# Delta-rule attention and a gated layer on one core: weight staging, a split of the recurrence's vector work, and a new instruction order

## The chip, the cores and the metric

The kernel runs on one core of a Trainium2 chip. The time is the device time of one execution in microseconds, of which the median of three runs is given. A core has the engines TensorE (PE in the profile, its weight loads PEld), VectorE (DVE), ScalarE (ACT), GpSimd (POOL) and SyncE (SP). Each executes its own instructions in order; SyncE, ScalarE and GpSimd also issue DMAs from their instruction streams, where an issue that has to wait holds up what stands behind it.

## The reference

```python
# q, k, v: (4, 8, 768, 48); beta: (4, 8, 768)
k_n = k / (np.linalg.norm(k, axis=-1, keepdims=True) + 1e-06)
for t in range(S):                       # state: (B, H, 48, 48), zero at first
    y[:, :, t] = q[:, :, t] @ state      # per batch and head
    v_old = state.T @ k_n[:, :, t]
    state += beta_t * outer(k_n_t, v_t - v_old)
x = y.transpose(0, 2, 1, 3).reshape(3072, 384)
h = x @ w_in                             # (384, 2048), float64 as given
out = (h * np.cos(h)) @ w_out            # (2048, 384), float64 as given
```

## The kernel before

**Tiling.** The sequence of 768 steps is cut into 24 units of 32 steps; a unit holds all four batches on 128 partitions (four quarters of 32) and eight heads beside each other. Two units make a pair of 256 tokens, the tile of the gated layer; there are 12 pairs.

**A unit of the recurrence** runs through: load k, q, v; transpose k and q (`turn`, units 0 to 5 on PE, later by `blocks` DMAs and a DVE transpose); Gram products of keys with keys and queries (`gram`); scale by beta over the squared norm (`gram_keys`), mask (`gram_queries`); invert the unit triangular matrix; then `through_state` (L930, k and q times the state), `right_side` (L947), `solve` (L1002), `solve_out` (L1014, which writes u twice, once for each half of the partitions' parity, by two multiplications with `bz`), `update` of the state (L1027) and `update_out` (L1035), `within` (L1045 for units 0 and 1, L1057 for later ones), `within_out` (L1070, four copies on ACT), `features` (L1078, transposes to tokens) and `features_out`.

**The inverses.** Units 0 and 1 are inverted by repeated multiplication on PE (`double`, L759, six levels with a copy on ACT, L767, and transposes and additions on DVE, L775, L772 and L779, between them). From unit 2 on the Gram block goes through DRAM (`gram_put`, L833; `gram_get`, L846/L854), is inverted column by column on GpSimd (L879, L886), and comes back through DRAM (`put`, L891; `get`, L902/L910). Units 2 and 3 are inverted in half blocks, with `solve_half` (L960), `between` and a last `solve` in place of one solve.

**The norms** of a pair's keys: a square on ACT (L557), a reduction on DVE (L562), a square root on GpSimd (L574), and five to six small DVE instructions (L591 to L598 for pairs 0 to 2, L603 to L611 later) that make `bs` and `bz`; `weigh` (L628) multiplies v by the norm.

**The gated layer.** Pair 0 is computed plainly: `hidden` (L1099) makes 512 hidden rows of 128 tokens as one block of 12 products, eight blocks in all; the gate takes two ACT (L1136, L1152) and two DVE instructions (L1143, L1155) for each; `output` (L1297) is eight blocks of four products. Later pairs use sums of weight and feature tiles to save products (`layer`, L1273; `product`, L1355), with sums of weight tiles made once by `in_sums` (L1235) and `right_sum` (L1384).

**The weights** arrive as float64 in 28 tiles (12 of w_in, 512 KB each; 16 of w_out, 384 KB each). `narrow_load` (L518) puts a tile into one of the eight g_ffn buffers, the same eight that hold gates, key squares and half solutions. Its words are turned into float32 by two ACT instructions (`split`, L528 and L532), one of DVE (`shift`, L536) and one of GpSimd (`add`, L540). A hidden block needs the adds of its tiles.

**The order.** Every step is a task with its engine; a list of task numbers, `Order.LINE`, written out in the source, fixes the order in which all tasks are issued, and so the order on each engine. The set `Order.OTHER` names tasks that run on their second engine: for a DMA the ScalarE queue in place of SyncE's, for a sum GpSimd and DVE exchanged. Costs and due times stand beside the tasks but only the list decides. Warm-up products (`keep_warm`, L495) are tasks like the others. Buffers are taken and given back in the list's order.

Of the kernel before, what the change touches and what calls it, by code (L numbers as in the profile page):

```python
# [10 lines left out]
FP = mybir.dt.float32  # L11
# [13 lines left out]
def _consts():  # L25

    p = np.arange(128)
    share = p // 64
    row = SPLIT * np.arange(C // SPLIT)[None, :] + share[:, None]
    return np.concatenate(
        [
            np.eye(128),
            p[:, None] % C < np.arange(C)[None, :],
            p[:, None] // C % 2 == np.arange(2)[None, :],
            p[:, None] // 16 % 2 == np.arange(2)[None, :],  # L40
            -1.0 * (p[:, None] // C % 2 == np.arange(2)[None, :]),
            (row[:, :, None] == np.arange(C)).reshape(128, -1),
        ],
        axis=1,
    ).astype(np.float32)


def _masks():
# [3 lines left out]
    other = ~side  # L52
    return np.concatenate(
        [(t < i) & (t // half == i // half), t // half < i // half]
        + [(s & x[:, None, :]).reshape(128, 2 * C) for s, x in ((side, t == i), (other, t < i))],
# [4 lines left out]
class Order:  # L60

    OTHER = {
        ('v', 0), ('v', 1), ('gram_put', 2), ('gram_put', 3), ('inv', 1, 0), ('put', 1),
        ('gram_put', 4), ('v', 5), ('gram_get', 2), ('put', 2), ('gram_put', 6), ('v', 8),
        ('v', 9), ('blocks', 9, 0), ('blocks', 9, 1), ('put', 4), ('get', 10), ('v', 11),
        ('blocks', 11, 0), ('blocks', 11, 1), ('gram_put', 11), ('gram_get', 5), ('v', 12),
        ('gram_put', 13), ('gram_get', 6), ('get', 13), ('v', 14), ('blocks', 14, 0), ('v', 15),
        ('blocks', 15, 0), ('blocks', 15, 1), ('v', 16), ('gram_put', 16), ('v', 17), ('k', 18),
        ('v', 18), ('get', 18), ('v', 20), ('gram_put', 21), ('gram_get', 11), ('store', 0, 1),
        ('right', 4, 4), ('left', 1, 1, 0), ('left', 1, 3, 0), ('left', 1, 3, 1),  # L70
        ('store', 1, 0), ('store', 1, 1), ('x_sum', 2, 'd'), ('x_sum', 2, 'n'),
        ('x_sum', 2, 'm'), ('x_sum', 2, 'e'), ('x_sum', 2, 'k'), ('x_sum', 2, 'g'),
        ('x_sum', 2, 'i'), ('x_sum', 2, 'l'), ('x_sum', 2, 'f'), ('x_sum', 2, 'b0'),
        ('left', 2, 4, 1), ('left', 2, 3, 1), ('x_sum', 3, 'd'), ('x_sum', 3, 'n'),
        ('x_sum', 3, 'm'), ('x_sum', 3, 'e'), ('x_sum', 3, 'k'), ('x_sum', 3, 'g'),
        ('x_sum', 3, 'i'), ('x_sum', 3, 'l'), ('x_sum', 3, 'h'), ('x_sum', 3, 'b0'),
        ('left', 3, 4, 1), ('left', 3, 3, 1), ('store', 3, 0), ('store', 3, 1),
        ('x_sum', 4, 'd'), ('x_sum', 4, 'm'), ('x_sum', 4, 'g'), ('x_sum', 4, 'i'),
        ('left', 4, 3, 0), ('left', 4, 3, 1), ('x_sum', 5, 'd'), ('x_sum', 5, 'e'),
        ('x_sum', 5, 'l'), ('x_sum', 5, 'h'), ('x_sum', 5, 'b0'), ('left', 5, 2, 0),  # L80
        ('left', 5, 4, 1), ('left', 5, 3, 0), ('left', 5, 3, 1), ('x_sum', 6, 'd'),
        ('x_sum', 6, 'g'), ('x_sum', 6, 'l'), ('x_sum', 6, 'f'), ('x_sum', 6, 'b0'),
        ('left', 6, 1, 0), ('left', 6, 4, 0), ('store', 6, 0), ('x_sum', 7, 'd'),
        ('x_sum', 7, 'm'), ('x_sum', 7, 'g'), ('x_sum', 7, 'i'), ('x_sum', 7, 'f'),
        ('x_sum', 7, 'h'), ('x_sum', 7, 'b0'), ('left', 7, 4, 0), ('left', 7, 4, 1),
        ('left', 7, 3, 1), ('store', 7, 0), ('x_sum', 8, 'd'), ('x_sum', 8, 'm'),
        ('x_sum', 8, 'e'), ('x_sum', 8, 'k'), ('x_sum', 8, 'g'), ('x_sum', 8, 'l'),
        ('left', 8, 3, 0), ('store', 8, 0), ('store', 8, 1), ('x_sum', 9, 'd'),
        ('x_sum', 9, 'm'), ('x_sum', 9, 'e'), ('x_sum', 9, 'k'), ('x_sum', 9, 'i'),
        ('x_sum', 9, 'l'), ('x_sum', 9, 'b0'), ('left', 9, 1, 0), ('left', 9, 2, 0),  # L90
        ('left', 9, 1, 1), ('left', 9, 3, 0), ('store', 9, 1), ('x_sum', 10, 'k'),
        ('x_sum', 10, 'i'), ('x_sum', 10, 'l'), ('x_sum', 10, 'h'), ('x_sum', 10, 'b0'),
        ('left', 10, 1, 0), ('left', 10, 1, 1), ('left', 10, 4, 1), ('left', 10, 3, 0),
        ('left', 10, 3, 1), ('store', 10, 1), ('x_sum', 11, 'd'), ('x_sum', 11, 'e'),
        ('x_sum', 11, 'k'), ('x_sum', 11, 'g'), ('x_sum', 11, 'f'), ('left', 11, 1, 0),
        ('left', 11, 2, 0), ('left', 11, 1, 1), ('left', 11, 3, 0), ('left', 11, 3, 1),
        ('store', 11, 1), ('store_right', 11), ('weights', 2), ('weights', 3), ('weights', 4),
        ('weights', 9), ('weights', 11), ('weights', 12), ('weights', 13), ('weights', 14),
        ('weights', 15), ('weights', 17), ('weights', 23), ('weights', 24)
    }  # L100

    WARM_FIRST, WARMS = 5, 17
    LINE = """
# [1845 lines left out]
```

## Time and profile before

| | |
|---|---|
| three runs | 640.14, 640.42, 641.46 us; median 640.42 |
| profiled execution, its own time | 642.77 us |
| its span, first to last instruction | 641.0 us |
| mean granted TensorE clock | 0.98 |
| HBM read and written | 38.95 MB and 10.22 MB |
| DMA packets | 215844, of them 207384 under 512 B |

A row of the timeline gives start and duration in microseconds, the engine, the source line, the operation, its output and input tiles with partitions x elements, a count, and in brackets the time for which the engine was idle before it and what released it. ACTq and SPq are the DMA issues in the streams of ScalarE and SyncE. A product in float32 leaves two records on PE, so a hidden block of 12 products is "x24". A row of groups (by line) gives the busy time, the mean in ns, and the idle time ahead. A row of windows gives a stretch, its length, then the busy time and the count for PE, PEld, DVE, ACT and POOL, the granted clock, the share of DMA time and GB/s. Ends of matmuls are modelled, so a busy PE is not PE at its peak.

### The profile page before, as it was taken

What the parts mean: (1) busy time and instruction counts of PE and PEld (TensorE: products, weight loads), DVE (VectorE), ACT (ScalarE), POOL (GpSimd) and SP (SyncE); (2) the same over time, 40 slices, a digit from 0 to 9 for tenths busy, and PEclk for the clock granted to TensorE, in tenths of its full rate; (3) what the DMA queues carried; (4) which work ended last, traced back from release to release, by engine and by line L of the source; (5) the groups of instructions that cost most, each with busy time, mean ns of one, the idle gap of its engine ahead of it and who ended that gap; (6) DMA issues with size and microseconds to landing.
All of it is one profiled execution on the core that took longest, in us unless ns stands there. A gap on an engine that the chain in (4) does not pass through costs nothing.

```text
span 641.0 us, 24058 instructions
## 1 busy us (share of the span) xinstructions
PE 612.1 (95%) x10096; PEld 571.4 (89%) x10096; DVE 504.4 (79%) x1051; ACT 297.5 (46%) x533; POOL 435.1 (68%) x791
## 2 busy tenths in 40 slices
PE   6978788999999999999999999999999999999997
PEld 4857777788799998999999999999999999999997
DVE  5876736999999897788878788978878676757872
ACT  3546535645543543543743553643544443635440
POOL 4428877788888888786886786888884881212231
PEclk8897979999999999999999999999999999999999
DMA  9876656655354645446234445333225011000001
GB/s 187 218 169 174 136 130 134 148 87 83 72 87 74 103 74 96 69 67 111 42 52 87 75 79 91 54 45 70 45 35 101 18 31 23 20 3 15 13 20 30
DMA packets 215844, 50.75 MB, mean 79 GB/s; under 512 B 207384, under 2 KB 210744, under 8 KB 215736
## 3 DMA queue, kind: packets, MB, share of 16 engines
q1 hardware_dynamic: 161132, 32.34, 27.8%
q10 hardware_dynamic: 54300, 16.33, 12.1%
q8 instruction: 79, 1.29, 0.8%
q0 software_dynamic: 304, 0.54, 0.4%
q14 instruction: 29, 0.24, 0.1%
HBM read 38.95 MB, written 10.22 MB: 77 GB/s over the span
## 4 chain that ended last, share of the span: by engine, by line
PE 76%; DMA 8%; POOL 5%; DVE 5%; issue 2%; SPq 2%; ACT 1%; ACTq 1%; DVEq 0%; POOLq 0%
PE p_out L1355 30%; PE p_h L1273 28%; PE p_kq L930 3%; PE p_s L1027 3%; POOL part L879 2%; POOL z L886 2%; PE p_u L1002 2%; PE p_kq L1057 2%; PE p_g L675 2%; PE p_h L1099 2%; DMA qp<-in_q_dram 2%; PE p_h L1355 2%; DMA kp<-in_k_dram 2%; PE p_z L1078 1%; DMA w_sum<-z_dr 1%
## 5 line engine op out<-in xcount | busy, mean ns | idle before, releaser
L879 POOL TENSOR_TENSOR part<-z,gb 128x126 f32<-128x126 f32 (+23 forms) x321 | 141.6, 441 | 44.1 <-DMA gb<-g_dr 17.5
L886 POOL TENSOR_TENSOR z<-z,part 128x126 f32<-128x126 f32 (+23 forms) x321 | 142.8, 445 | 25.2
L1355 PE MATMUL p_out<-w_out,g_ffn 128*128 128x192 f32 x672 | 121.0, 329 | 0.0
L1355 PEld LDWEIGHTS p_out<-w_out,g_ffn 128*128 128x128 f32 x672 | 107.9, 190 | 1.0
L1152 ACT ACTIVATE turns<-turns,halfpi 128x512 f32<-128x512 f32 x96 | 68.0, 718 | 83.2 <-DVE turns L1143 71.6
L1273 PE MATMUL p_h<-x_sum,w_in 128*128 128x128 f32 x704 | 92.3, 278 | 0.0
L1355 PE MATMUL p_out<-w_sum,g_ffn 128*128 128x192 f32 x496 | 88.7, 328 | 0.0
L1273 PEld LDWEIGHTS p_h<-x_sum,w_in 128*128 128x128 f32 x704 | 85.6, 191 | 1.9
L1136 ACT ACTIVATE turns<-g_ffn,quarter_turn 128x512 int32<-128x512 f32 x77 | 55.0, 719 | 66.3 <-DVE g_ffn L1155 35.4
L1355 PEld LDWEIGHTS p_out<-w_sum,g_ffn 128*128 128x128 f32 x496 | 79.6, 190 | 0.6
L1290 DVE TENSOR_TENSOR g_ffn<-g_ffn,p_h 128x512 f32<-128x512 f32 x88 | 59.5, 679 | 14.7 <-PE p_h L1273 13.7
L1155 DVE TENSOR_TENSOR g_ffn<-turns,g_ffn 128x512 f32<-128x512 f32 x77 | 61.7, 810 | 11.7 <-ACT turns L1152 11.6
L1143 DVE SCALAR_TENSOR_TENSOR turns<-g_ffn,turns 128x512 f32<-128x512 f32 x77 | 57.1, 750 | 8.2 <-ACT turns L1136 8.1
L1273 PE MATMUL p_h<-x_sum,in_sum 128*128 128x128 f32 x440 | 58.9, 278 | 0.8 <-POOL x_sum L1188 0.8
L1273 PEld LDWEIGHTS p_h<-x_sum,in_sum 128*128 128x128 f32 x440 | 54.3, 191 | 2.2 <-POOL x_sum L1188 1.0
L1070 ACT COPY y<-p_kq 32x384 f32<-32x384 f32 x96 | 45.1, 470 | 19.0 <-PE p_kq L1057 8.1
L1407 DVE SCALAR_TENSOR_TENSOR o<-p_out,o 128x192 f32<-128x192 f32 x74 | 25.1, 351 | 29.7 <-PE p_out L1355 29.5
L1273 PE MATMUL p_h<-x_ffn,w_in 128*128 128x128 f32 x352 | 46.6, 277 | 1.0 <-ACT p_h L1285 1.0
L1273 PEld LDWEIGHTS p_h<-x_ffn,w_in 128*128 128x128 f32 x352 | 43.0, 192 | 1.6 <-ACT p_h L1285 1.3
L574 POOL TENSOR_TENSOR knrm<-ksum,halves 128x16 f32<-128x16 f32 (+1 forms) x14 | 37.1, 2647 | 10.1 <-DVE ksum L562 9.5
L1371 POOL TENSOR_TENSOR g_ffn<-g_ffn 128x512 f32<-128x512 f32 x15 | 19.1, 1271 | 30.5 <-DVE g_ffn L1155 26.6
L1285 ACT COPY p_h<-p_h 128x512 f32<-128x512 f32 x44 | 25.3, 575 | 28.5 <-PE p_h L1273 20.4
(168 smaller groups left out, 1051.7 us busy)
## 6 DMA issues: line engine op xcount, KB each, us to landing
g_ffn<-in_moe_w_in_dram SPq DMA_DIRECT2D x7, 512.0 KB, 7.8
g_ffn<-in_moe_w_out_dram SPq DMA_DIRECT2D x9, 384.0 KB
kp<-in_k_dram SPq DMA_DIRECT2D x136, 24.0 KB, 2.5
gb<-g_dr SPq DMA_DIRECT2D x12, 256.0 KB, 3.9
g_ffn<-in_moe_w_out_dram ACTq DMA_DIRECT2D x7, 384.0 KB
g_ffn<-in_moe_w_in_dram ACTq DMA_DIRECT2D x5, 512.0 KB, 5.9
vp<-in_v_dram ACTq DMA_DIRECT2D x52, 48.0 KB, 2.7
zt<-z_dr SPq DMA_DIRECT2D x68, 32.0 KB, 2.7
```

Source lines behind the costliest of these rows:

```text
L574: nc.gpsimd.tensor_tensor(out=scales[m][2][:, part], in0=sums[m, part.start][:, 0:n], in1=halves[:, 0:n], op=ALU.pow,)
L879: eng.tensor_tensor(out=part, in0=z[:, 0:rows, j, None].to_broadcast(shape), in1=a[:, j, None, j + 1 :].to_broadcast(shape), op=ALU.mult,)
L886: eng.tensor_tensor(out=behind, in0=behind, in1=part, op=ALU.subtract)
L1070: nc.scalar.copy(by_parity(y[quarter(b)]), p_kq[quarter(b ^ 1), :, b % 2])
L1136: nc.scalar.activation(turns[p, f], hidden_of(p, f), AF.Identity, bias=quarter_turn, scale=TURN)
L1143: nc.vector.scalar_tensor_tensor(out=r, in0=hidden_of(p, f), scalar=TURN, in1=t, op0=ALU.mult, op1=ALU.subtract,)
L1152: nc.scalar.activation(r, r, AF.Sin, bias=halfpi, scale=2.0 * math.pi)
L1155: nc.vector.tensor_tensor(out=place(p, f), in0=step_of(rests.pop((p, f)), f), in1=step_of(hidden_of(p, f), f), op=ALU.mult,)
L1273: nc.tensor.matmul(p_h[:, e], in_block(*w)[:, e], x_of(p, b), start=new and e == 0, stop=True, skip_group_check=True,)
L1285: nc.scalar.copy(to, part_of(p, one))
L1290: nc.vector.tensor_tensor(out=part_of(p, to), in0=part_of(p, one), in1=part_of(p, two), op=op)
L1355: nc.tensor.matmul(p_o, left(p, part, a)[:, e % 4], right(e, b), start=(e == 0), stop=(e == FT // 2 - 1), skip_group_check=True,)
```

## The change

**Weight staging.** Tiles 0 to 5 (of w_in) and 12 to 15 (of w_out) are loaded into the place that w_out will fill; tiles 16 to 27 into w_sum, once unit 1 has been solved; only tiles 6 to 11 still use g_ffn buffers. Loads and splits wait for the adds of tiles that were staged in the same place.

```diff
+    def stage_of(t):
+        if t < 6:
+            return "out", 1024 * t, 1024 * t + 1024
+        if t < 12:
+            return None
+        if t < 16:
+            return "out", 3072 + 768 * (t - 12), 3840 + 768 * (t - 12)
+        return "sum", 768 * (t % 4), 768 * (t % 4) + 768
...
     def narrow_load(t):
-        words[t] = g_home("pairs", t).bitcast(U32)[:, 0 : 2 * n]
+        words[t] = staged(t).bitcast(U32)[:, 0 : 2 * n]
```

**Pair 0 in pieces.** `hidden` becomes four tasks of three products each, `output` four tasks of one product each for every former block. The products are the same.

```diff
-            add(layered[0], "PE", 2.62, lambda f=f: hidden(p, f), deps,
+            for i in range(4):
...
+                add(layered[0], "PE", 0.66, lambda f=f, i=i: hidden(p, f, i), deps,
```

**Norms.** From pair 1 on, the square and its sum over 48 columns are one ACT instruction per unit and head with an accumulator (8 or 16 instructions); the reduction on DVE goes. ACT also squares the norm plus 1e-6 and copies the norms for `weigh` (`norms_out`); DVE keeps the reciprocal and one product.

```diff
+        if m > 0:
+            for i in range(n):
+                for h in range(H):
+                    nc.scalar.activation(
+                        square, kps[m % len(kps)][:, part.start + i, h, 0:D], AF.Square,
+                        accum_out=ksum[:, i, h : h + 1],
+                    )
+            return
...
+        nc.scalar.activation(krec, knrm, AF.Square, bias=tiny)
```

**u.** From unit 2 on, DVE writes u once (one instruction instead of two, half the elements); `within` reads it, and two ACT instructions make the two copies that `update` reads. `within` no longer waits for `update`.

```diff
+    def part_out(n):
+        u = parts[n] = work.tile([128, H, 2, D], FP, name="u", bufs=1)
+        for x in range(2):
+            nc.scalar.activation(u[:, :, x], us[n], AF.Copy, scale=odd[:, x : x + 1])
```

**Smaller edits.** Units 0, 1, 4 and 5 are solved in quarters (32 products of 32x48 in place of 16 of 64x48), and units 0 and 1 use the same quarter form of `within` as the others, with one DVE instruction for the masked queries instead of two. `double_rest` is cut into `double_eye` and `double_far`, of which unit 0's two and unit 1's second run on GpSimd. `right_side` has three DVE instructions instead of four. For units 0 to 3 half of `within_out` is a task of its own (`within_half`, on DVE for units 0 and 1, on ACT for 2 and 3). The identity of the GpSimd inverse is read from a 62-column constant that is loaded later, from SyncE. The table load of ACT stands behind four instead of eight DMA issues. Three sums of weight tiles go to GpSimd, and ten of eleven feature sums of pair 1 to DVE.

**The order.** `Order.LINE` and `Order.OTHER` are new lists; 22 instead of 17 warm-up tasks, besides the five at the start. In ScalarE's stream the first DMA issue behind the loads of k and q stands now behind the first five weight splits; the loads of weights 0 to 6, of v and the gram stores of units 2 to 5 are issued by SyncE, put 1 by ScalarE. The split of weight tile 1 stands ahead of unit 0's first doubling copies, the split of tile 2 ahead of its second ones. On PE, unit 0's six levels are no longer interleaved evenly with those of unit 1, whose last three levels come after unit 0's solve. `features` 0 follows `within` 0 directly, and hidden pieces stand in runs of one to five between the steps of units 1 to 3.

475 lines of the change are left out of this document (269 added, 206 removed), and 204 rows, old and new, of the table LINE.

## The prediction

> **What bounds the kernel now.** I read the profiled execution by stage first: the busy totals, then a table of windows (columns: length, busy time and count of PE, PEld, DVE, ACT, POOL, clock, DMA share, GB/s).
>
> ```profile
> span 641.0 us, 24058 instructions
> PE 612.1 (95%) x10096; PEld 571.4 (89%) x10096; DVE 504.4 (79%) x1051; ACT 297.5 (46%) x533; POOL 435.1 (68%) x791
> ```
> ```profile
> 6.00:58.70 52.70, 40.62 (x928) 34.15 (x926) 41.11 (x123) 29.05 (x59) 24.07 (x27) 0.87 0.78 193
> 58.70:112.00 53.30, 43.74 (x1057) 40.14 (x1052) 31.48 (x66) 26.24 (x52) 42.82 (x82) 0.90 0.64 139
> 112.00:190.00 78.00, 76.75 (x1245) 64.18 (x1247) 74.81 (x145) 40.38 (x73) 66.33 (x116) 1.00 0.54 95
> 190.00:640.00 450.00, 446.37 (x6878) 429.04 (x6870) 354.22 (x708) 201.85 (x350) 297.77 (x557) 1.00 0.32 55
> ```
>
> Two regimes. From 112 us on TensorE is idle 1.3 us up to 190 and 3.6 us from there to the end, at full clock: there only TensorE's own work can shorten the run. From 6 to 112 us it is idle 12.1 + 9.6 = 21.7 us, with a mean clock of 0.87 and 0.90. All that this change can win lies ahead of 112 us, where the first units' recurrence runs as one chain through PE, DVE, ACT and the DMA queues and too little feed-forward work is ready to fill the holes. Whatever the chain gains there, the packed rest starts earlier by.
>
> The next view is the order of time in that head; start, duration, engine, and in brackets the idle time before and its releaser.
>
> ```profile
> 17.98 2.21 ACTq L398 DMA_DIRECT2D vp<-in_v_dram  x3
> ...
> 21.52 0.69 ACT L528 ACTIVATE w_in<-g_ffn 128x512 f32<-128x512 f32 x1 [3.26 <-DMA vp<-in_v_dram]
> ...
> 43.27 2.17 ACTq L833 DMA_DIRECT2D g_dr<-g  x2
> 45.48 0.37 ACT L767 COPY in_sum<-p_h 128x256 f32<-128x256 f32 x1 [7.37 <-DVE w_in L536]
> ```
> ```profile
> 25.93 1.96 PE L759 MATMUL p_h<-in_sum 64*64 64x128 f32 x32
> ...
> 46.89 1.32 PE L1002 MATMUL p_u<-vp,in_sum 64*64 64x48 f32 x32 [0.30 <-ACT kq_t L652]
> ...
> 58.71 4.75 PE L1099 MATMUL p_h<-x_ffn,w_in 128*128 128x128 f32 x24
> 63.40 1.13 PE L1002 MATMUL p_u<-rhs,w_sum 64*64 64x48 f32 x32
> ...
> 82.71 1.54 PE L960 MATMUL p_w<-rhs,w_sum 32*32 32x48 f32 x60 [0.81 <-DMA w_sum<-z_dr]
> ...
> 86.30 4.62 PE L1099 MATMUL p_h<-x_ffn,w_in 128*128 128x128 f32 x24
> 90.85 0.88 PE L996 MATMUL p_u<-g_ffn,w_sum 32*32 32x48 f32 x64
> 91.66 2.94 PE L1099 MATMUL p_h<-x_ffn,w_in 128*128 128x128 f32 x24
> 94.53 0.89 PE L1027 MATMUL p_s<-u,kp 64*64 64x96 f32 x32
> ...
> 99.48 1.15 PE L930 MATMUL p_kq<-st,kq_t 48*64 48x48 f32 x64
> ```
>
> Twice ScalarE stands still behind DMA issues in its own instruction stream (3.26 and 7.37 us) while copies of the doubling chain wait behind them; solve 0 comes at 46.89 us, the first hidden block at 58.71. Later, whole blocks of 12 products (24 records, 2.94 us at full clock, 4.62 and 4.75 at half) stand between the short steps of units 2 and 3: between their correction and their solve, and between solve and state update.
>
> **The change part by part.** I write the steps as a sum against the profiled 642.77 us (span 641.0, 1.8 outside it); the median shown is 640.42, 2.35 less.
>
> *Up to solve 1.* The weights no longer wait for a g_ffn buffer, so they go out from SyncE's queue and the two early stalls of ScalarE's queue go; the matrices of two inverse steps go to GpSimd; one unit's bz and half of two queries leave DVE. Against that stand the following prices.
>
> ```profile
> L536 DVE TENSOR_SCALAR w_in<-w_in 128x512 uint32<-128x512 uint32 x12 | 4.8, 411 | 0.0
> L562 DVE TENSOR_REDUCE ksum<-g_ffn 128x8 f32<-128x384 f32 (+1 forms) x6 | 4.1, 682 | 5.4 <-ACT g_ffn L557 5.4
> L779 DVE TENSOR_TENSOR in_sum<-in_sum,p_h 128x256 f32<-128x256 f32 x8 | 3.3, 412 | 3.1 <-PE p_h L759 2.1 <-ACT in_sum L767 1.0
> ...
> L775 DVE STREAM_TRANSPOSE in_sum<-p_h 128x256 f32<-128x256 f32 x6 | 2.7, 443 | 0.7 <-PE p_h L759 0.6
> ...
> L628 DVE SCALAR_TENSOR_TENSOR vp<-knrm,vp 128x768 f32<-128x768 f32 x2 | 1.9, 968 | 1.3 <-DMA qp<-in_q_dram 1.3
> ```
> ```profile
> L528 ACT ACTIVATE w_in<-g_ffn 128x512 f32<-128x512 f32 x12 | 8.2, 684 | 4.6 <-DMA vp<-in_v_dram 3.3 <-DMA qp<-in_q_dram 0.7 <-POOL part L879 0.6
> L528 ACT ACTIVATE w_out<-g_ffn 128x384 f32<-128x384 f32 x12 | 6.6, 549 | 0.0
> L652 ACT COPY kq_t<-p_t 128x512 f32<-128x512 f32 x12 | 6.4, 588 | 6.0 <-PE p_t L642 3.9 <-DMA g_ffn<-in_moe_w_in_dram 2.1
> ```
> ```profile
> 8.21 0.20 ACT L461 ACTIVATE warm<-halfpi 128x1 f32<-128x1 f32 x1
> ...
> 48.13 0.87 ACT L557 ACTIVATE g_ffn<-kp 128x768 f32<-128x768 f32 x1
> ```
> ```profile
> g_ffn<-in_moe_w_in_dram SPq DMA_DIRECT2D x7, 512.0 KB, 7.8
> ```
>
> In the new order of ScalarE the split of weight tile 1 stands ahead of the first copies of the doubling. Its load is issued near 11 us; with 7.8 us to landing and two halves of some 0.65 it ends near 20, so the second level starts at 20.6 us. Before the third level stand a copy of k and q (1.2), eight squares (1.6, below), another split (1.3) and a copy (0.4) on ScalarE, then turn 3 (1.1) on PE: the third level starts near 28.7, where the old one started at 25.93, so 2.8 us later. From there to the last addition DVE is the chain: seven transposes at 0.44, eight additions and two products of gram blocks of the same size at 0.41, four shifts at 0.41, one weigh (0.97), and five small ones of a fold and a scale that I put at 1.3 together: 11.1 us in all, from 30.3 to 41.4. Solve 0 follows at about 42.2 against 46.89: -4.7. The old stretch from the third level to solve took 21 us because of the 7.37 us stall and because both inverses were carried side by side. After solve 0 the new order puts update, within and features directly behind; half of the copy of y goes to DVE, so the first hidden piece comes near 49 against 58.71. But 5.5 us of unit 1's doubling, turn 4, gram 4 and state 1 are then still ahead, so the gain that holds is that at solve 1: I get 58.5 against 63.40. **-5** for this stage, between 0 (should the early weight tile come 5 us later than its median) and -8.
>
> *The squares with a sum on ScalarE.* A pair's one square (0.87) and its sums on DVE (0.68 in the mean) become 16 activations of 48 columns with an accumulator, not in the trace of before. From below they cost 0.13 each, the slope between 128x256 and 128x512 rows carried to 48 columns; from above 0.37, the 128x256 copy. I take 0.20, the nearest row (128x1): 3.2 us instead of 0.87. In the head eight of them stand on the chain twice (counted above); in the packed stage ScalarE is busy 201.85 of 450 us and takes 2.3 more per pair, 1.9 for the split of u (two activations of 384 columns per unit) and 0.9 for small copies: some 5 us in 44, which its idle half hides. Were that cover gone, PE would wait up to 2.3 us per pair, 23 us over ten pairs; I take +0.5.
>
> The Trainium skill's page "ScalarE: Activation LUTs", section "What ACT_TABLE_LOAD costs", gives 186 ns + 0.833 ns per column with some 93 ns of overlap; by it 16 squares take an estimated 2.2 us, and the sum would differ by under 1 us. Its "Rules for kernel authors" gives additions and products to VectorE, which speaks against this part; the trace says that DVE, 74.81 busy of 78 us between 112 and 190, is the fuller of the two.
>
> *Units 2 and 3.* The inverse of unit 2 arrives by eight DMAs that stand behind a gram store in SyncE's queue.
>
> ```profile
> 71.98 5.06 SPq L902 DMA_DIRECT2D w_sum<-z_dr  x8
> ```
>
> That order stays, so p_w of unit 2 moves with the chain, from 82.71 to about 78. Behind it the hidden work comes in pieces of three products (0.73 us). Between the correction and solve 2 one piece remains of 4.5 us of block, saving 3.7; between solve and update two pieces and the new u copy (1.0) replace 2.94 and a 1.0 us u: saving 0.5 to 1; and the 2.94 us block that stood behind the update ahead of state 3 goes, within now standing before update: 2. State 3 then stands at 88 to 90 against 99.48. Unit 3 repeats it, but from there PE runs out of holes: between 49 us and solve 3, I count some 42 us of PE work in the new order, so the chain's further lead is capped by PE. What counts is the idle time removed: of 9.6 us between 58.7 and 112, I take back 6, of the half-clock loss (two blocks by 1.7 us each) 1.5. The rest stays, as the inverse of units 4 and 5 (30 us of GpSimd) starts only 2.5 us earlier. **-7.5**, between -2 and -11.
>
> *TensorE's own work.*
>
> ```profile
> 66.43 1.51 PE L1045 MATMUL p_kq<-u,zt 64*64 64x96 f32 x32
> ...
> 95.36 0.88 PE L1057 MATMUL p_kq<-u,tt 32*32 32x48 f32 x64
> ```
> ```profile
> 134.86 1.16 PE L1273 MATMUL p_h<-x_sum,in_sum 128*128 128x128 f32 x8
> 135.85 1.06 PE L1273 MATMUL p_h<-x_ffn,w_in 128*128 128x128 f32 x8
> 136.75 1.06 PE L1273 MATMUL p_h<-x_ffn,in_sum 128*128 128x128 f32 x8
> ```
>
> Two within steps take 64 small records instead of 32 wide ones, -0.6 each, and four solves likewise, -0.25 each: -2.2. A layer behind another shape starts its successor after 0.99 us, behind its own shape after 0.90, so a change of shape costs 0.1; the pieces add about 22 such changes among hidden and 8 among output: +3. The five more warm-up products only fill idle time. **+0.8.** DVE's savings in the packed stage (some 3 us a pair) are worth nothing there, as PE is the bound.
>
> Sum: -5 - 7.5 + 0.8 + 0.5 = -11.2, of which I keep 10 (the steps overlap where PE is already full): 632.8 for the profiled execution, 630.4 against the median. **I predict 630.5 us.**
>
> **The rivals.** (1) *Little gain*: the early weight tiles delay ScalarE's copies (the split standing in front) and the crowded DMA (share 0.78 between 6 and 58.7) delays k and q, and solve 1 stays near 63; what units 2 and 3 win is given back where solve 4 waits for GpSimd's inverse, which starts hardly earlier: 635 to 641. For it: 7.8 us to landing; against it: buffers free from the start. (2) *Slower*: ScalarE becomes the serial engine. If the 16 squares take over 0.3 us each (4.8 us a pair, and 10 us with the rest), they push part_out, which now stands between solve and update, and the layer copies; the update is placed in PE's order as if they were short, and PE waits. It decides from about 1 us of wait per unit on: 20 units, +20, less 10 from the head, gives 650. Against it: PE waited for ACT hardly at all after 190 us. (3) *Packed head*: from 49 us on PE has no hole and stays at full clock: 582 us of the old run lie behind its first hidden block, less 12 idle, 5 of half clock and 1 of work, plus 5.5 us of work moved behind it: about 571 after 49, thus 620 and the median at 619. For it: pieces of 0.73 us fit any hole. (4) The change does what it says, by the built order; that isn't in doubt.
>
> ```profile
> 84.00:88.00 4.00, 3.38 (x84) 3.07 (x74) 1.47 (x4) 2.58 (x5) 3.30 (x10) 0.50 0.92 274
> ```
>
> Half clock was granted right behind the long holes, as in this row behind the wait for z_dr. The Trainium skill's "TensorE: Matmul & The Clock Gate", Part 1, says that an idle window of about 3.4 us brings the half rate and a sustained busy one ends it; by that rule rival 3 takes its 5 us back as well, and the trace agrees so far.
>
> **How the numbers follow.** Forecast (-5 to -16 us) 0.60; little gain 0.16, of which a third within 0.2%; packed 0.12; slower 0.12. A measurement of this kernel can tell 0.2% (1.3 us) from no change. Faster: 0.60 + 0.12 + 0.10 = 0.82; same 0.06; slower 0.12. The range leaves out half of the packed case and the slower one: 619 to 642. The likeliest case alone spans 624 to 635.
>
> **What would show it.** Right: solve 0 at 40 to 44 us, the first hidden piece before 51, solve 1 near 58.5, state 3 before 91, no ACT idle over 3 us before a doubling copy, idle PE under 13 us between 6 and 112, and from 112 on PE as full as now. Wrong: doubling copies waiting for a split; squares over 0.3 us; idle PE named after ACT u behind 190 us; PE waiting for zt at solve 4 by more than 3 us.

## The result and the profile after

The changed kernel takes 647.56 us in the median of seven runs (646.38 to 653.62), the kernel before 641.26 (637.67 to 644.14): ratio **1.011**, interval 1.007 to 1.015. It is slower by 1.1%; 630.5 us was forecast. The profiled execution took 646.41 us, that of before 642.77.

First the page's totals of the kernel after, then its windows with the same borders as in the prediction (length, busy time and count of PE, PEld, DVE, ACT, POOL, clock, DMA share, GB/s).

```profile
span 644.6 us, 24744 instructions
...
PE 613.1 (95%) x10296; PEld 568.4 (88%) x10296; DVE 475.1 (74%) x931; ACT 374.1 (58%) x950; POOL 429.7 (67%) x787
...
6.00:58.70 52.70, 42.24 (x1033) 36.34 (x1033) 40.62 (x107) 37.40 (x122) 32.71 (x43) 0.97 0.85 206
58.70:112.00 53.30, 46.45 (x1168) 39.27 (x1161) 36.29 (x67) 37.03 (x106) 42.97 (x75) 0.97 0.64 130
112.00:190.00 78.00, 75.36 (x1409) 63.65 (x1411) 70.06 (x132) 50.82 (x137) 63.55 (x115) 1.00 0.56 100
190.00:640.00 450.00, 443.59 (x6688) 425.49 (x6689) 324.98 (x614) 247.34 (x588) 286.93 (x546) 1.00 0.31 53
```

Length less PE's busy time is its idle time. Up to 112 us it fell from 12.08 + 9.56 to 10.46 + 6.85 us: **-4.3**. Behind 112 us it was 1.25 + 3.63 before, of which 2.66 lie behind the last product (the old run ends at 641.0 with 3.65 us of tail), so 2.2; after it is 2.64 + 6.41 = 9.05 with no tail in it: **+6.8**. Busy time rose by 1.0, start and tail by 0.2. Together +3.7, and the span grew by 3.6.

Busy time alone hides the clock, which differs between the two traces. PE was granted half clock in these stretches, first before, then after:

```profile
11.33:21.57 10.24, 7.11 (x124) 5.77 (x124) 9.21 (x27) 2.20 (x6) 4.57 (x6) 0.50 0.82 174
55.70:62.53 6.83, 6.83 (x105) 6.19 (x102) 5.25 (x16) 4.16 (x9) 5.58 (x17) 0.50 0.66 176
83.01:89.84 6.83, 6.21 (x138) 5.90 (x134) 2.15 (x7) 2.58 (x5) 5.58 (x17) 0.50 0.89 254
```
```profile
16.06:19.48 3.42, 3.42 (x90) 3.12 (x85) 2.38 (x8) 2.64 (x10) 3.19 (x3) 0.50 0.78 141
108.22:111.64 3.42, 3.42 (x11) 2.21 (x10) 2.23 (x5) 3.24 (x15) 2.87 (x8) 0.50 1.06 273
384.70:388.12 3.42, 3.42 (x14) 3.42 (x14) 1.74 (x3) 1.82 (x3) 3.33 (x4) 0.50 0.34 54
```

An estimate from them: a hidden block of 24 records takes 2.94 us at full clock and 4.75 at half, so a busy microsecond at half clock is worth 0.62 at full. At full clock PE's work would then be 604.5 us before and 609.2 after: **+4.7**, not +1.0. The slower clock cost 5.1 us less up to 112 us and 1.3 more behind it. The balance of the two traces is then, in the head, -4.3 idle and -5.1 clock; behind 112 us, +6.8 idle and +1.3 clock; in PE's own work, wherever it lies, +4.7; start and tail, +0.2.

So the change is ahead at 112 us: PE has 519.7 us of busy time left there (75.36 and 443.59, and 0.80 behind 640 us), and the kernel before 523.1. It loses the lead behind 112 us, where it stands idle for 6.8 us more.

The medians differ by 6.3 us, 2.7 more than the traced executions. The clock can account for that: the kernel before had a mean granted clock of 0.987 in 74 executions beside the experiments and 0.980 in the traced one, the change 0.989 in 13 executions and 0.992 in the traced one. So most of the clock's gain belongs to the two executions that were traced.

The order of time on PE (start, duration, engine, line, operation, output and inputs, and in brackets the idle time ahead with its releaser):

```profile
41.19 0.88 PE L1039 MATMUL p_u<-vp,in_sum 32*32 32x48 f32 x64 [0.80 <-DVE in_sum L822]
...
48.69 0.91 PE L1159 MATMUL p_h<-x_ffn,w_in 128*128 128x128 f32 x6
...
58.55 0.29 PE L1039 MATMUL p_u<-rhs,w_sum 32*32 32x48 f32 x8
...
88.17 1.15 PE L965 MATMUL p_kq<-st,kq_t 48*64 48x48 f32 x64
...
383.65 1.16 PE L1333 MATMUL p_h<-x_sum,in_sum 128*128 128x128 f32 x8 [1.94 <-ACT p_h L1345]
384.64 2.70 PE L1414 MATMUL p_out<-w_sum,g_ffn 128*128 128x192 f32 x8
387.14 1.52 PE L1333 MATMUL p_h<-x_ffn,w_in 128*128 128x128 f32 x8
388.50 1.47 PE L1414 MATMUL p_out<-w_sum,g_ffn 128*128 128x192 f32 x8
```

Solve 0 at 41.19 (46.89 before, 42.2 forecast), first hidden piece at 48.69 (58.71; 49), solve 1 at 58.55 (63.40; 58.5), state 3 at 88.17 (99.48; 88 to 90). Every milestone came within about 1 us of the forecast, and the kernel is slower. The last four rows show a new sight, a layer that waits 1.94 us for a copy on ScalarE; behind the wait one block of eight products takes 2.70 us, where the next takes 1.47.

What PE waited for behind 112 us (in total, times, longest), first after, then before:

```profile
PE p_h L1333 <- ACT p_h L1345: 2.6, 2, 1.9
PE p_out L1414 <- DVE o L1466: 2.0, 4, 1.0
PE p_h L1333 <- ACT g_ffn L1345: 1.1, 3, 0.7
PE p_u L1044 <- DMA zt<-z_dr: 1.0, 2, 0.8
```
```profile
PE p_h L1273 <- ACT p_h L1285: 1.0, 1, 1.0
PE p_h L1273 <- POOL x_sum L1188: 0.8, 1, 0.8
```

And what ScalarE did ahead of the 1.94 us, with its two groups for the squares (count, busy time, mean ns, idle time ahead):

```profile
L587 ACT ACTIVATE square<-kp 128x48 f32<-128x48 f32 x176 | 42.7, 243 | 6.5 <-DMA kp<-in_k_dram 1.4
L587 ACT ACTIVATION_READ_ACCUMULATOR square<-kp 128x1 f32 x176 | 32.8, 187 | 0.0
...
376.66 0.25 ACT L587 ACTIVATE square<-kp 128x48 f32<-128x48 f32 x1
376.81 0.19 ACT L587 ACTIVATION_READ_ACCUMULATOR square<-kp 128x1 f32 x1
377.03 0.24 ACT L587 ACTIVATE square<-kp 128x48 f32<-128x48 f32 x1
...
382.17 0.24 ACT L587 ACTIVATE square<-kp 128x48 f32<-128x48 f32 x1
...
383.02 0.57 ACT L1345 COPY p_h<-p_h 128x512 f32<-128x512 f32 x1
```

An activation with an accumulator is two instructions, and one square comes every 0.37 us (376.66, 377.03): the 16 of a pair hold ScalarE for 5.9 us in one piece, and the copy that PE needs stands behind them.

### The profile page after: what moved, and what is told of

Its sections match the earlier page's. It is cut to its first block, busy times and chain, and to the rows that moved or that the text cites. A ratio compares the mean times of both kernels' runs of the same rounds, so it can differ in the third digit from the quotient of the medians.

```text
span 644.6 us, 24744 instructions
## 1 busy us (share of the span) xinstructions
PE 613.1 (95%) x10296; PEld 568.4 (88%) x10296; DVE 475.1 (74%) x931; ACT 374.1 (58%) x950; POOL 429.7 (67%) x787
## 5 line engine op out<-in xcount | busy, mean ns | idle before, releaser
L914 POOL TENSOR_TENSOR part<-z,gb 128x126 f32<-128x126 f32 (+23 forms) x321 | 139.9, 436 | 37.9 <-ACT z L902 9.9
L1414 PE MATMUL p_out<-w_sum,g_ffn 128*128 128x192 f32 x496 | 90.0, 331 | 1.7 <-DVE o L1466 1.7
L1215 DVE TENSOR_TENSOR g_ffn<-turns,g_ffn 128x512 f32<-128x512 f32 x77 | 57.4, 751 | 12.7 <-ACT turns L1212 12.6
L1116 ACT COPY y<-p_kq 32x384 f32<-32x384 f32 x88 | 41.4, 470 | 13.3 <-PE p_kq L1103 7.1
L1430 POOL TENSOR_TENSOR g_ffn<-g_ffn,g_ffn 128x512 f32<-128x512 f32 x12 | 16.2, 1354 | 48.1 <-PE p_out L1414 28.1
L587 ACT ACTIVATE square<-kp 128x48 f32<-128x48 f32 x176 | 42.7, 243 | 6.5 <-DMA kp<-in_k_dram 1.4
L1333 PEld LDWEIGHTS p_h<-x_ffn,w_in 128*128 128x128 f32 x352 | 44.4, 194 | 2.3 <-ACT p_h L1345 1.0
```

The costliest lines, as they stand in the source:

```text
L587: nc.scalar.activation(square, kps[m % len(kps)][:, part.start + i, h, 0:D], AF.Square, accum_out=ksum[:, i, h : h + 1],)
L914: eng.tensor_tensor(out=part, in0=z[:, 0:rows, j, None].to_broadcast(shape), in1=a[:, j, None, j + 1 :].to_broadcast(shape), op=ALU.mult,)
L1116: nc.scalar.copy(by_parity(y[quarter(b)]), p_kq[quarter(b ^ 1), :, b % 2])
L1215: nc.vector.tensor_tensor(out=place(p, f), in0=step_of(rests.pop((p, f)), f), in1=step_of(hidden_of(p, f), f), op=ALU.mult,)
L1333: nc.tensor.matmul(p_h[:, e], in_block(*w)[:, e], x_of(p, b), start=new and e == 0, stop=True, skip_group_check=True,)
L1414: nc.tensor.matmul(p_o, left(p, part, a)[:, e % 4], right(e, b), start=(e == 0), stop=(e == FT // 2 - 1), skip_group_check=True,)
```

## The experiments

All ratios are to the kernel before, measured in the same runs on the same chip. Each kernel has one trace, of one execution; that of the change again shows how far two executions of one kernel differ: its idle time is 14.1 us up to 112 us (17.3 in the first trace), 4.3 between 112 and 190 (2.6) and 6.1 behind (6.4).

| kernel | ratio | interval |
|---|---|---|
| the change | 1.011 | 1.007 to 1.015 |
| the change again | 1.013 | 1.009 to 1.016 |
| 1 squares on one instruction, sums late | 1.055 | 1.051 to 1.059 |
| 2 copies of u by VectorE | 1.024 | 1.022 to 1.027 |
| 3 both | 1.054 | 1.051 to 1.057 |
| 4 before, with the accumulators alone | 1.078 | 1.075 to 1.081 |
| 5 squares in one instruction, sums early | 1.014 | 1.009 to 1.018 |
| 6 as 5, accumulators up to pair 3 | 1.011 | 1.007 to 1.015 |
| 7 split of u undone | 1.019 | 1.016 to 1.023 |
| 8 as 5 and 7 | 1.014 | 1.009 to 1.018 |
| 9 as 5, accumulators up to pair 5 | 1.008 | 1.005 to 1.011 |
| 10 pieces put together | 1.020 | 1.016 to 1.023 |
| 11 before, gram stores 2 and 3 by SyncE | 1.000 | 0.998 to 1.002 |
| 13 as 9, with local fixes | 1.005 | 1.002 to 1.009 |
| 14 the change, with the queue edit | 1.012 | 1.008 to 1.016 |
| 15 as 13, pair 4 without accumulators | 1.009 | 1.006 to 1.012 |
| 16 as 13, pairs 4 and 5 without | 1.007 | 1.004 to 1.009 |

**1, 2 and 3.** The first theory: the squares hold ScalarE, and PE waits behind them. The rival: the new order itself costs.

```diff
+            if m > 0:
...
+                nc.scalar.square(ksq[:, 0:n], kps[m % len(kps)][:, part, :, 0:D])
+                return
...
     def norms_root(m, part):
...
+        if m > 0:
+            nc.vector.tensor_reduce(
+                out=sums[m, part.start][:, 0:n], in_=squares.pop((m, part.start))[:, 0:n],
+                axis=mybir.AxisListType.X, op=ALU.add,
+            )
```

> The changed kernel, with the squares of pairs 1 to 11 in one ScalarE instruction again and their sums on VectorE; everything else as changed (the square of pair 9 stands a little later so that a buffer is free for it). In the trace after, each of the 176 squares is followed by a second ScalarE instruction that reads the accumulator (0.187 us), one square comes every 0.366 us, and a pair holds ScalarE for 5.9 us in one piece. Theory (the squares hold ScalarE, and TensorE waits behind them): idle TensorE behind 112 us, 9 us in the trace after and 2.2 before, falls to 3 or less, and the time falls by 5 to 8 us, to 640 to 643. Rival (the new order itself costs: more changes between layers, products and steps of the recurrence, TensorE busy 613.1 instead of 612.1 us): the time stays within 2 us of the changed kernel, 646 to 649.

```diff
-            nc.scalar.activation(u[:, :, x], us[n], AF.Copy, scale=odd[:, x : x + 1])
+            nc.vector.tensor_scalar(u[:, :, x], us[n], odd[:, x : x + 1], None, op0=ALU.mult)
```

> The changed kernel, with the two copies of u per unit (two activations of 384 columns, 1.1 us) written by VectorE in place of ScalarE, at the same place of the order. Theory (the squares are the cost): ScalarE gets back 1.1 us per unit, but not where the 5.9 us blocks stand, and the time changes by -2 to +1 us. Rival (the copy between solve and update is the cost): idle TensorE ahead of the updates and layers goes and the time falls by 4 us or more.

> Both together: squares of pairs 1 to 11 in one instruction with their sums on VectorE, and the two copies of u by VectorE; ScalarE then carries what it carried before, except for the small norms. Theory: as the kernel with the squares alone, or up to 2 us below it, 639 to 643. Rival of the order: within 2 us of the changed kernel. Should VectorE be the bound instead (475 us busy after, 504 before), this one is slower than each of the two alone.

Theory and rival both missed 1.055. The sum stood at the place of the square root in the order, where VectorE's stream lags behind GpSimd's; GpSimd's waits in the first kernel:

```profile
POOL knrm L631 <- DVE ksum L621: 40.5, 9, 10.6
```

So this kernel measured a badly placed sum, not the squares. The second missed both of its forecasts too (1.024). In it the update waited for the copies, although VectorE is free for 26% of the span in the kernel after:

```profile
PE p_s L1086 <- DVE u L1077: 4.5, 5, 1.5
```

Its 21 us of added VectorE time cost some 8 us. The third is no slower than the first alone (1.054 and 1.055), so it says nothing further.

**4.** The accumulators alone, in the order of before.

```diff
     def norms_square(m, part):
...
+        if m > 0:
...
+            for i in range(n):
+                for h in range(H):
+                    nc.scalar.activation(
+                        square, kps[m % len(kps)][:, part.start + i, h, 0:D], AF.Square,
+                        accum_out=ksum[:, i, h : h + 1],
+                    )
+            return
```

> The kernel before with one part of the change alone: the squares of pairs 1 to 11 as 16 ScalarE activations per pair (8 per unit in pair 1) with an accumulator, no sum on VectorE; order, u and weights as before. Theory: the old order has no place for 5 us more on ScalarE per pair in one piece, and the time rises by 4 to 10 us, to 645 to 651. Rival of the order: ScalarE is busy 297 of 641 us and takes 60 more in its idle time, so the time stays within 1.5 us of the kernel before.

+50 us, five times the theory's upper end. 176 squares every 0.366 us add 64 us, and 9 us of wide squares go: 55 us of added ScalarE time, in a kernel in which ScalarE was busy for 46%, came out as 50. Part of it is clock: 0.947 granted in its trace, 0.980 in that of before. PE's waits, and the worst of them in time:

```profile
PE p_h L1286 <- ACT p_h L1298: 15.2, 4, 8.9
PE p_h L1286 <- ACT g_ffn L1300: 14.8, 3, 8.8
...
354.15 2.08 PE L1286 MATMUL p_h<-x_sum,in_sum 128*128 128x128 f32 x8 [8.88 <-ACT p_h L1298]
```

In this order the squares of two pairs follow each other (32 between 340.8 and 352.9 us), and a layer copy stands behind them. Idle time of an engine in order is no reserve for work that is put ahead of a copy that another engine awaits. That the change pays so much less for the same squares suggests that its order had found better places for them.

**5 to 8.** The sum where VectorE arrives about 1 us after the square begins.

```diff
+        for k, ahead in sums.items():
+            line.insert(line.index(ahead), ("sum",) + k)
```

> The changed kernel with the squares of pairs 1 to 11 in one ScalarE instruction and their sum on VectorE, as in the first experiment, but the sum now stands in the order at the place that VectorE reaches about 1 us after the square begins, not at GpSimd's square root, where GpSimd waited 40 us for it. ScalarE gets back 5 us per pair, VectorE takes 0.94 us more. Theory (blocks of 5.9 us on ScalarE are what TensorE waits for behind 112 us): idle TensorE behind 112 us falls from 9 to 4 us or less, ratio to the kernel before 0.995 to 1.004 where the changed kernel has 1.011. Rival (the new order has found places for these blocks, and its cost is elsewhere): ratio 1.008 to 1.02, as the sums now push VectorE's later work.

> The same, but pairs 1 to 3, whose squares stand ahead of 75 us, keep the 16 activations with an accumulator; pairs 4 to 11 have one square and a sum on VectorE. It tells where the squares cost. Theory: they cost in the packed stage, so this one is within 2 us of the kernel with all squares in one instruction. Rival: they cost in the chain of the first units (ScalarE stands between the doubling steps), and this one is 3 us or more slower than that kernel.

In 7 the constant decides from which pair on u is split; below it VectorE writes both halves of u by `bz`, as before.

```diff
-    SPLIT_U = 1
+    SPLIT_U = 12
...
-            add(ready, "ACT", 1.0, lambda: part_out(n), [("solve_out", n)],
-                makes=[("u", ("u", n))], uses=[("u_all", n)])
+            add(ready, "ACT", 1.0, lambda: None, [("solve_out", n)])
```

> The changed kernel with the split of u undone from unit 2 on: VectorE writes both halves of u from the solution by two instructions with bz, as before, ScalarE writes no copies, within reads the same u; bz costs VectorE one small instruction per pair. Squares as changed. Between solve and update stand then two VectorE instructions of some 0.55 us in place of one and two of ScalarE. Theory (squares are the cost, the split is harmless): the time stays within 3 us of the changed kernel, ratio 1.006 to 1.016. Rival (the copies by ScalarE between solve and update are the cost): ratio 1.003 or less. Writing the two copies on VectorE on top of its own instruction made it slower by 8 us; if VectorE's added time is waited for in the same way here, ratio 1.015 to 1.025.

> Both: squares in one instruction with early sums on VectorE, and u written by VectorE as before. ScalarE then carries what it carried before, the order is the new one. Theory: the squares' gain and the u's change add up, ratio 0.995 to 1.006. Rival of the order: ratio 1.008 or more, as the order's own cost stays.

Without the 16 squares the time did not fall (5), nor with u as before too (8, where the rival holds): the theory as it stood is wrong. 6 came 2.6 us below 5, between its two forecasts. Its windows, with accumulators up to pair 3, suggest why there is no gain:

```profile
112.00:190.00 78.00, 71.61 (x1289) 59.39 (x1289) 68.55 (x128) 42.52 (x83) 62.20 (x111) 1.00 0.56 98
190.00:640.00 450.00, 446.62 (x6813) 428.77 (x6814) 332.37 (x630) 223.40 (x405) 294.36 (x555) 1.00 0.32 55
```

Behind 190 us PE's idle time fell from 6.41 to 3.38; between 112 and 190 us it rose from 2.64 (4.3 in the second trace of the change) to 6.39, now with waits for VectorE's state, right side and gates: there the sums, on the fuller engine, seem to cost what the squares had cost. The split of u is not the cost but worth some 5 us beside the accumulators (1.019 without it against 1.011 and 1.013); with the squares in one instruction it is worth nothing (5 and 8, both 1.014).

**9, 10, 11 and 12.** Accumulators only where VectorE is full; the pieces joined; the prediction's own reckoning, by one edit to the kernel before; the change again.

```diff
+            if m not in (1, 2, 3, 4, 5):
```

> The changed kernel with its squares with an accumulator up to pair 5, and one square with a sum on VectorE from pair 6 on (behind 190 us). With all or most squares in one instruction, idle TensorE behind 190 us fell from 6.4 to 2.7 and 3.4 us, but between 112 and 190 us, where VectorE is the fuller engine, it rose from 2.6 to 7.3 and 6.4, and the total stayed. Theory: the squares cost 3 us behind 190 us and the sums on VectorE 4 us ahead of it, so this kernel has both gains: idle TensorE behind 112 us 6 us or less, ratio to the kernel before 1.002 to 1.008. Rival (any VectorE work added to this order is waited for, early or late): ratio 1.010 or more.

```diff
     def hidden(p, f, i):
...
+        if i < 3:
+            return
+        for i in range(4):
```

> The changed kernel with the pieces of pair 0 put together again: hidden blocks of twelve products and output blocks of four, each at the place of its last piece. Theory (the pieces cost more on TensorE than they fill): output took 23.2 us in 18 runs where before it took 21.0 in 7, and the pieces' changes of shape cost 2 to 4 us, so the ratio falls to 1.003 to 1.008. Rival (the pieces fill the holes between the short steps of units 1 to 5): without them idle TensorE ahead of 112 us rises from 18.7 to 25 us or more, and the ratio is 1.015 or more.

```diff
-        ('v', 0), ('v', 1), ('gram_put', 2), ('gram_put', 3), ('inv', 1, 0), ('put', 1),
+        ('v', 0), ('v', 1), ('inv', 1, 0), ('put', 1),
```

> The kernel before with one edit: the gram stores of units 2 and 3 are issued by SyncE in place of ScalarE, so that the stall of 7.4 us in ScalarE's stream ahead of a doubling copy (38 to 45 us) goes. It tests the reckoning of the prediction by which a lead of the chain at its solve is a gain of the whole run. By that reckoning: solve 0 comes some 4 to 6 us earlier than at 46.89 us and the time falls by as much, ratio 0.991 to 0.994. Rival (TensorE was busy with unit 1 and warm-up through most of the stall, 3 us idle in 38 to 50 us, and only that idle time can go): solve 0 comes earlier by as much, but the time falls by 2 us or less, ratio 0.997 to 1.003.

> The changed kernel once more, beside the other three on the same chip. Expected: ratio 1.009 to 1.014, as the kernel differs from the kernel before by 1.1% with an interval of 0.7 to 1.5%; idle TensorE behind 112 us 9 us as in its first trace, if those waits are the kernel's own and not those of one execution.

9: 644.44 against 647.9 us of the change in the same runs, so the squares behind pair 5 cost some 3.5 us. The two intervals overlap by 0.001, but the 1.94 us wait at 383.65 us is gone in its trace and stands in both traces of the change. Idle PE behind 112 us is 7.8 us, more than the 6 expected, and less than in the change (9.0 and 10.4; 12 had expected 9). 10: the pieces are no cost either; joined, the time rises by 4 us. The rival's mechanism holds, its place only partly: idle time up to 112 us is 19.8 (17.3 and 14.1 with pieces), not 25, and between 112 and 190 us it is 6.2:

```profile
6.00:58.70 52.70, 40.92 (x984) 34.71 (x984) 39.44 (x103) 35.49 (x118) 32.16 (x41) 0.90 0.86 195
58.70:112.00 53.30, 45.24 (x1178) 40.37 (x1176) 31.74 (x58) 33.40 (x90) 38.34 (x66) 0.94 0.61 120
112.00:190.00 78.00, 71.77 (x1268) 60.04 (x1271) 65.38 (x128) 52.88 (x148) 57.91 (x108) 0.98 0.58 103
```

11 prices the stall. The wait of 7.37 us is gone. The doubling copy it held, and solves 0 and 1 on PE with the block ahead of solve 1:

```profile
42.83 0.37 ACT L767 COPY in_sum<-p_h 128x256 f32<-128x256 f32 x1 [3.74 <-PE p_h L759]
...
45.91 1.14 PE L1002 MATMUL p_u<-vp,in_sum 64*64 64x48 f32 x32 [0.55 <-ACT kq_t L652]
...
56.94 2.94 PE L1099 MATMUL p_h<-x_ffn,w_in 128*128 128x128 f32 x24
59.81 1.14 PE L1002 MATMUL p_u<-rhs,w_sum 64*64 64x48 f32 x32
```

ScalarE now waits 3.74 us for PE instead: the copy was not due before 42.8 us, so of the 7.37 us only 2.65 (45.48 less 42.83) had delayed it. Solve 0 comes 1.0 us earlier, not the 4 to 6 that both theories put there. The time does not change (1.000, interval 0.998 to 1.002), so the theory's 0.991 to 0.994 is wrong. Solve 1 comes 3.6 us earlier, but 1.8 of that is the block ahead of it, 2.94 us here and 4.75 at half clock in the trace before. Nor is it a lead without a gain: the span of this trace is 636.7 us against 641.0, while the two medians agree. What this run shows is that the stall was worth about 1 us; whether a larger lead would have been kept it does not show.

**13 to 16.** What is left of the loss.

```diff
-        ('gram_get', 3), ('v', 9), ('gram_get', 4), ('put', 4), ('blocks', 10, 1),
+        ('gram_get', 3), ('v', 9), ('put', 4), ('blocks', 10, 1),
...
-        ('weights', 13), ('weights', 14), ('weights', 17), ('weights', 23)
+        ('weights', 13), ('weights', 14), ('weights', 17)
```

> The kernel with accumulators up to pair 5 only (ratio 1.0075), with two more edits. The load of weight tile 23 and the reading of gram 4 are issued by SyncE in place of ScalarE: in its trace ScalarE stands behind these two issues until GpSimd is done (1.1 us at 107, 3.1 us at 125), and TensorE waits 2.0 and 1.8 us for the copies behind them. And the sum of pair 7 stands two VectorE steps later, where it does not wait 1.8 us for its square. Theory (what is left of the loss is local waits behind ScalarE's stream): idle TensorE behind 105 us falls from 9.8 to 6 us or less and the ratio to 1.001 to 1.005. Rival (SyncE's queue then holds up the loads of k, q and v behind the two issues, or the loss is TensorE's own work): ratio 1.007 or more.

> The changed kernel with the queue edit alone (weight tile 23 and gram 4 issued by SyncE). Theory: the wait of 2 to 2.7 us for the copy of y at 108 us goes, and the ratio falls by 0.002 to 0.004 from 1.0126, to 1.009 to 1.011. Rival: TensorE waits for the same copies through another engine (VectorE is the fuller one there), ratio 1.012 to 1.014.

> The kernel with the local fixes (ratio 1.005), with the squares of pair 4 too in one instruction and a sum on VectorE. In the trace of that kernel the 16 squares of pair 4 hold ScalarE from 106.5 to 112.2 us; TensorE waits 2.2 us for the layer copy behind them, VectorE 1.9 us for a weight split behind them, and half clock follows. Theory (one block of squares, one wait): this wait goes, idle TensorE behind 105 us falls by 2 us or more, and the ratio by 0.003 or more, to 1.002 or less. Rival (the sum of pair 4 delays VectorE's chain to the state update by as much, as in the kernel with accumulators up to pair 3): ratio 1.004 or more.

> The same with pair 5 too in one instruction and a sum; it is the kernel with accumulators up to pair 3 (ratio 1.0106, made with other places for two sums) plus the local fixes. Theory (the queue stalls made that kernel's waits at 106 to 127 us): ratio 1.002 or less. Rival (VectorE is full between 112 and 190 us and each sum there is waited for): 1 to 4 us slower than the kernel with pair 5's accumulators.

13 came to 1.005, at the edge of the theory's range, and its interval overlaps that of 9; idle time behind 105 us fell to 6.7 us, not 6. Its largest wait behind 112 us is again one behind 16 squares, those of pair 4, which end at 112.2 us, and four weight splits that follow them:

```profile
112.23 0.53 ACT L559 ACTIVATE w_out<-w_sum 128x384 f32<-128x384 f32 x1
...
114.61 1.70 PE L1352 MATMUL p_h<-x_sum,w_in 128*128 128x128 f32 x8 [2.18 <-ACT g_ffn L1366]
```

Taking that block away too (15, 16) did not help: idle time between 112 and 190 us went from 3.9 to 7.5 and 5.5 us, with waits for VectorE and for other copies. In 15 the rival holds (1.009). In 16 neither does: 1.007, and 1.2 us faster than 15, where the rival had it slower. 14 can't be told from the change by its time, and shows a wait that moved: with the issues gone from ScalarE's stream, a weight split in it waits 5.91 us for its own load, the copy to x_ffn stands behind it, and PE behind that:

```profile
101.61 0.54 ACT L555 ACTIVATE w_out<-w_sum 128x384 f32<-128x384 f32 x1 [5.91 <-DMA w_sum<-in_moe_w_out_dram]
...
103.51 0.45 ACT L1146 COPY x_ffn<-p_z 128x384 f32<-128x384 f32 x1
...
104.02 0.86 PE L721 MATMUL p_g<-kq_t 48*32 48x64 f32 x64 [2.32 <-ACT x_ffn L1146]
```

No version tried beats the kernel before.

## Why the prediction was wrong

Two steps failed outright: "from 112 us on PE as full as now", and "TensorE's own work: +0.8". A third, the squares, was mis-sized. The two steps of the head came out smaller than forecast, but within their ranges in the traces.

**"Up to solve 1: -5."** Its times came true (solve 1 at 58.55). PE's idle time up to 58.7 us fell by only 1.6 us; by the estimate above, half clock cost 2.5 us less there, 4.1 in all. Part of that is the execution that was traced: of the 4.85 us by which solve 1 came earlier, 1.8 are the old block ahead of it at half clock, which is at full clock in the trace of experiment 11 too, without the change. The stall that the step named as cause was read wrongly: a copy that waits 7.37 us behind a DMA issue is late only by what it waits beyond its own input, here 2.65 us (experiment 11). Its way to the third level does not add up either: the terms named come to 5.6 us, and from 20.6 to 28.7 are 8.1.

**"Units 2 and 3: -7.5."** Wrong in size. State 3 came at 88.17 as forecast, but of the 9.6 us of idle time 2.7 went, not 6; half clock cost some 2.5 us less by the estimate, where 1.5 were forecast: 5.2 in all. The sign set for the head, idle PE under 13 us between 6 and 112, did not come: it is 17.3 us, and 14.1 in the second trace.

**"Squares with a sum on ScalarE: +0.5."** Mis-sized. The single square was put at 0.20 us from a row without an accumulator, with 0.37 as the upper bound; it takes 0.37 with the second instruction that the estimate did not know of. (The lower bound of 0.13 does not follow from the two copy rows, 0.37 and 0.588, whose slope gives 0.19 at 48 columns.) By the Trainium skill's page "ScalarE: Activation LUTs", section "What ACT_TABLE_LOAD costs", 16 squares were estimated at 2.2 us; measured are 5.9, and the page's figures hold for the first of the two instructions only (243 ns; 186 + 0.833 x 48 = 226). The squares behind pair 5 cost some 3.5 us (experiment 9). The idle half of ScalarE did not hide them, since they stand ahead of copies that PE awaits.

**"From 112 us on PE as full as now."** This step failed, and with it the forecast: PE stood idle for 6.8 us more, and ran at half clock behind one wait. Some 3.5 us are the squares of pairs 6 to 11, by the times; the rest are short waits for ScalarE's copies and VectorE's outputs, between which no single edit decided. That VectorE's saved time is worth nothing looks wrong as well between 112 and 190 us: sums of 0.94 us put back there (experiments 5, 6, 15, 16) left 1.6 to 4.7 us more idle time on PE in spite of the freed ScalarE; these are single traces, and the two of the change differ by 1.7 us there.

**"TensorE's own work: +0.8."** This looks near, as busy time rose by 1.0, but that is luck: less half clock hides an estimated 4.7 us of added work. The same estimate gives 604.1 us for the trace of experiment 11, which has the products of before, and 609.6 for the change again. The changes of shape were counted for pair 0 alone. In the traces its hidden pieces stand in 20 runs (8 before) and its output pieces in 17 (7), so 22 more in all where 30 were counted; but the layers of the later pairs stand in 140 runs instead of 127 and take 235.9 us for the same 1760 records, 233.9 before. Warm-up products take 14.5 us against 12.9 (48 records against 40). They fill idle time, as the step says, but then that idle time is no gain either. The output pieces show how a mean misleads; the row of the kernel after, where the mean was 488 ns before, and the four records that raise it most:

```profile
L1356 PE MATMUL p_out<-w_out,g_ffn 128*128 128x384 f32 x64 | 25.5, 520 | 0.0
...
108.41 2.77 PE L1356 MATMUL p_out<-w_out,g_ffn 128*128 128x384 f32 x4
```

64 records at 32 ns more are 2.0 us, but 1.4 of them are these four, at half clock behind a wait of 2.71 us; the median is 486 ns in both kernels. Joined, the mean is 489 ns (experiment 10); yet the pieces as a whole are worth 4 us in this order.

**The rivals.** Rival 2 had the sign, the threshold and the place: squares over 0.3 us ahead of the layer copies. Its price, 1 us per unit and 20 in all, was too high, and part_out, which it named too, made PE wait 0.2 us. Its gain of 10 us in the head is 4.3 of idle time and an estimated 5.1 of clock in the traces, and less in the medians. Rivals 1 and 3 are refuted by the milestones and by the idle time; the terms of rival 3 add up to 570 us, not 571. The rule on the clock that the prediction cites with rival 3 fits the wait for z_dr in the kernel before, but not the kernel after, where half clock also followed a wait of 1.94 us in an otherwise full stretch, shorter than the idle window that it names.

**Still open.** With the squares as before from pair 6 on and the local fixes, 0.5% (0.2 to 0.9%) stays above the kernel before. PE's work in the new order is there in its trace (609.2 us at full clock by the estimate, against 604.5 before), and would be enough; but its idle time there is less than before, and how far the order's own small waits add to it in other executions the runs do not tell. The new head with the old order behind 112 us was not tried.

## What to carry to other kernels

Count a lead of a dependency chain as a gain only by the idle time and half clock that it takes from the bounding engine, and price the stretch behind it with the same care: here the head's lead was lost there. Compare busy times at equal clock, and a trace with its own median, before reading a few microseconds out of them. In streams that run in order, the free share of an engine hides nothing by itself: ask which awaited instruction stands next behind the added work. An edit of an engine's work and a fixed instruction order belong together, so a part tried alone in an order made for another can cost many times what it costs in its own (50 us for eleven pairs, against some 3.5 for the last six).

## What the runs showed of the hardware

- An activation with an accumulator leaves a second instruction on ScalarE, 187 ns beside 243 for 48 columns, one pair every 0.37 us.
- After some waits of about 2 us PE ran at half clock for 3.4 us, as in this row of the kernel after, behind the 1.94 us wait at 383.65 us; a short wait can so cost nearly as much again. It does not always follow: in both traces of the change PE waits 2.44 us ahead of the first features (near 45 us), and half clock follows in the second (47.65 to 51.06 us) and not in the first. Executions of one kernel differ by this.

```profile
384.00:388.00 4.00, 4.00 (x21) 4.00 (x19) 2.44 (x5) 1.82 (x3) 3.21 (x4) 0.59 0.47 75
```

- Sums of weight tiles on VectorE, 679 ns at best, took up to 1507 in the kernel after, where weight additions of 1.0 us each ran on GpSimd at the same time:

```profile
L1295 DVE TENSOR_TENSOR in_sum<-w_in x3: 679/1494/1507, 69.6 to 101.2; 128x512 f32<-128x512 f32 x3
```

The Trainium skill's page "SBUF — State Buffer", section "SBUF: two separate sides", says that the two engines share a pair of ports which one holds for a whole instruction while the other waits, among other cases when a VectorE instruction with two SBUF inputs meets a GpSimd one that reads SBUF. This row agrees.
